# First products of small blocks in two halves of their columns, in an attention and mixture-of-experts kernel

## The chip, the core and the metric

The kernel runs on one core of a Trainium2 chip. The metric is the device time of one execution in microseconds. A core has five engines with a program each: TensorE (PE: matrix products, and PEld: loads of their weights), VectorE (DVE), ScalarE (ACT), GpSimd (POOL) and SyncE (SP, which issues most transfers). An engine runs its program in order and waits on counters (semaphores) for the others. PEldq and ACTq are the engines' sequencers.

## The reference

Two stages, in float32:

```
attn = sigmoid(q @ k.T / sqrt(64) - log(448)) @ v     # 8 x 12 heads of 448 x 64
x = attn, laid out as 3584 tokens x 768
for the tokens with x @ w_skip > 0:
    e = argmax(x @ w_gate) of 8 experts, g = its softmax weight
    x += g * (relu(x @ w1[e]) @ w2[e])                 # w1 768 x 1024, w2 1024 x 768
```

## The kernel before

After attention the tokens are sorted by expert into blocks. A loop of 14 rounds (`tc.For_i`, line 1553) takes one block a round and picks one of four arms by a word from `slots` (`choose`, 1541 to 1550):

- FULL and SPLIT take 128 rows. Each weight is held as a high and a low part, and a product is three matmuls: first product line 516, turning of h line 530, second product line 547. SPLIT belongs to the last full block of an expert and also splits the next expert's raw weights: high parts by ACT (lines 1252 and 1258), low parts by DVE.
- HALF takes up to 64 rows and FEW up to 32, at an expert's end. They use the raw float32 weights (`raw1`, `raw2`) and lay two (HALF, 64 columns each) or four (FEW, 32 each) products side by side on PE (matmuls of lines 1474 and 1416).

The order is written out by hand (`tc.manual_schedule`): each engine's program follows the text. By the start of their first product in the trace, the rounds are SPLIT 313.64, HALF 332.25, FULL 344.48, HALF 363.03, FULL 375.25, FEW 393.81, FULL 400.80, FEW 419.36, FULL 426.34, FEW 444.90, SPLIT 451.91, FEW 470.42, FULL 477.46, FEW 496.00. One HALF and one FEW follow a SPLIT, one HALF and four FEW a FULL.

A small block runs so: the first product `xf @ w1` into the bank `ph[0]`, six steps j of 128 input rows each; ACT's relu into `hs`, in column pieces (lines 1433, 1489); loads of the next w1 (`load_w1`, SP); six turns of the next block's rows `xn` on PE (`turn_x`, line 492, into `pxt`); the turns of h on PE (lines 1442, 1497) into `pht[0]` and `ph[1]`; ACT's copies of these to `ht` (lines 1444, 1503); `ready_x`, which makes the next block's `xh`, `xl` and `xf`; the second product into `py`, from `ht` and `raw2`; the weighting, the scatter of the rows, and the records of the next block. `ph[0]` and `ph[1]` are tiles of their own, `pht[0]` and `pht[1]` two banks of one tile, `pht2`. `xf` is written by ACT (`whole_x`, line 1116).

The program of PE is aligned once, ahead of the loop, by `addr_align` (line 1158), to a place in a fetch block of instructions.

Of the kernel before, what the change touches and what calls it, by code (L numbers as in the profile page):

```python
# [14 lines left out]
AF = mybir.ActivationFunctionType  # L15
# [4 lines left out]
P = 128  # L20
# [3 lines left out]
def kernel(  # L24
# [11 lines left out]
    nc = tc.nc  # L36
# [11 lines left out]
    NK1 = DM // P  # L48
    NK2 = FF // P
    H1 = FF // 2  # L50
# [6 lines left out]
    SM = 32  # L57
# [15 lines left out]
    ident = const.tile([P, P], F32, name="ident")  # L73
# [174 lines left out]
    def new_t(name):  # L248

        if ps_t is None:  # L250
            return new_s(name)[:, 0, :]
        return ps_t.tile([P, 512], F32, tag="t", name=name)
# [236 lines left out]
    def turn_x(x, h, px):  # L489
        for j in range(3):  # L490
            i = 3 * h + j
            nc.tensor.transpose(  # L492
                px[:, j * P : (j + 1) * P], x[:, i * P : (i + 1) * P], ident
            )
# [192 lines left out]
    for n, (b, hp) in enumerate(steps):  # L687
# [39 lines left out]
        for c in range(4):  # L727
            at = wk.tile([P, 2, S], F32, tag="A", name=f"at_{b}_{hp}_{c}", bufs=5)
# [83 lines left out]
    def new_ph(j):  # L812
        one = new_s(f"b{j}_ph")
        return [one[:, 0, :], ps_b.tile([P, 512], F32, tag="b", name=f"b{j}_ph1")]
# [4 lines left out]
    def turn0(h):  # L819
        pt = new_t(f"b0_pht{h}")  # L820
        for j in range(4):
            nc.tensor.transpose(
                pt[:, j * P : (j + 1) * P], hs0[h][:, j * P : (j + 1) * P], ident
            )
        split_h(h, pt, hh0, hl0)
# [28 lines left out]
    ph = new_ph(0)  # L854
# [13 lines left out]
    xf = rows_pool.tile([P, NK1, MD], F32, name="xf")  # L868
    ys = rows_pool.tile([P, DM], F32, name="ys")
    ht = rows_pool.tile([P, 4 * P], F32, name="ht")  # L870
    hs = rows_pool.tile([P, FF], F32, name="hs")
# [202 lines left out]
    ph = new_ph(1)  # L1074
# [49 lines left out]
    def ready_x():  # L1124
        for h in range(2):
            hi_x(h, pxt[h], xh)
        for h in range(2):
            whole_x(h, [slice(j, j + 1) for j in range(3)])
        for h in range(2):
            lo_x(h, pxt[h], xh, xl)  # L1130
# [24 lines left out]
    for j in range(2):  # L1155
        gemm2(j, hh0, hl0, py)
    turn0(1)
    nc.tensor.addr_align(bass.FETCH_BLOCK_INSTRUCTIONS, offset=0, max_nops=0)
    for j in range(2, NK2 - 3):
        gemm2(j, hh0, hl0, py)  # L1160
    pxt = [ps_b.tile([P, 512], F32, tag="b", name="pxt0"), new_t("pxt1")]
# [60 lines left out]
    raw1 = [[raw1g[h, i // 3][:, i % 3, :] for h in range(2)] for i in range(NK1)]  # L1222
    raw2 = [raw2g[j // 2][:, j % 2, :] for j in range(NK2)]

    ph = [new_t(f"ph{h}") for h in range(2)]
    py = new_s("py")
    pht2 = new_s("pht")
    pht = [pht2[:, h, :] for h in range(2)]

    def next_expert(word):  # L1230
        return word & (NE - 1), (word & (2 * NE)) >> (2 * NE).bit_length() - 1

    def load_w1(g, h, nx):
        return nc.sync.dma_start(
            raw1g[h, g],
            w1[ds(nx[0], 1), g * 3 * P : (g + 1) * 3 * P, h * H1 : (h + 1) * H1].rearrange(
                "o (i p) f -> p (o i) f", p=P
            ),
            cond=nx[1],
        )  # L1240
# [42 lines left out]
    def fetch():  # L1283


        pool.tensor_tensor(xn[:, 0:1], xn[:, 0:1], zf, op=ALU.add)
        pool.tensor_tensor(jk, rn[:, 0:2], rn[:, 0:2], op=ALU.add)
        pool.tensor_copy(ri, rn[:, 1:2])
        pool.tensor_tensor(rn[:, 0:1], rn[:, 0:1], zf, op=ALU.add)
        pool.tensor_tensor(rx, rix[:, 5:6], zero, op=ALU.add)  # L1290
        pool.tensor_tensor(rp[1], ri, zero, op=ALU.add)
        pool.tensor_tensor(rq, rp[1], zero, op=ALU.add)
        got = gather(xn, rp[1])

        tc.declare_no_dep(got.ins, group="put", across_iterations=True, reason="a token is in one block only")
        tc.add_to_no_dep_group("got", got.ins)
        gather_rec(rn, rx)

    def shift(eng):
        for to, src in ((riv, rix[:, 6:NS]), (rix[:, 5 : NS - 1], riv)):  # L1300
            if eng is pool:
                eng.tensor_tensor(to, src, zero.to_broadcast([P, NS - 6]), op=ALU.add)
            else:
                eng.tensor_copy(to, src)
# [39 lines left out]
    def take_rec():  # L1344

        nc.vector.tensor_copy(recs[:, 2, 0:2], rn[:, 0:2])
# [61 lines left out]
    def few(i, word):  # L1408

        nx = next_expert(word)  # L1410
        for o in range(2):
            nc.vector.tensor_copy(gate2[o * SM : (o + 1) * SM], recs[:SM, 0, 0:1])  # L1412
        take_rec()

        def quarter(dst, g, n, a, w, j, most):
            nc.tensor.matmul(  # L1416
                dst[g * SM : (g + 1) * SM, :n],
                a,
                w,
                start=(j == 0),  # L1420
                stop=(j == most - 1),
                tile_position=(0, g * SM),
            )

        Q1 = FF // 4
        for j in range(NK1):
            for g in range(4):
                s = slice((g % 2) * Q1, (g % 2 + 1) * Q1)
                quarter(ph[0], g, Q1, xf[:, j, :SM], raw1[j][g // 2][:, s], j, NK1)
        turned = (pht[0], ph[1])  # L1430
        parts = [slice(c * P, (c + 1) * P) for c in range(2)]
        for s in parts:
            nc.scalar.activation(hs[:, s], ph[0][:, s], AF.Relu)
        for h in range(2):
            for g in range(2):
                load_w1(g, h, nx)
        for h in range(2):
            turn_x(xn, h, pxt[h])
        fetch()
        ht4 = ht[:, : 8 * SM].rearrange("p (c g t) -> p c g t", c=2, g=4)  # L1440
        for s, p in zip(parts, turned):
            nc.tensor.transpose(p[:, :P], hs[:, s], ident)
        for s, p in zip(parts, turned):
            nc.scalar.activation(ht[:, s], p[:, :P], AF.Copy)
        ready_x()
        shift(dve)

        for n, j in enumerate((0, 2, 1, 3)):
            for g in range(4):
                h, o = g // 2, g % 2  # L1450
                m = j + h * (NK2 // 2)
                quarter(
                    py[:, 0, :],
                    g,
                    H2,
                    ht4[:, j % 2, 2 * h + j // 2, :],
                    raw2[m][:, o * H2 : (o + 1) * H2],
                    n,
                    NK2 // 2,
                )  # L1460
        for g in range(4):
            load_w2(g, nx)
        nc.scalar.activation(yh, py[MD:, 0, :H2], AF.Copy, scale=gate2)
        nc.vector.scalar_tensor_tensor(yt, py[:MD, 0, :H2], gate2, yh, op0=ALU.mult, op1=ALU.add)
        put(SM)
        advance()

    def half(i, word):

        nx = next_expert(word)  # L1470
        take_rec()

        def side(dst, g, n, a, w, j, most):
            nc.tensor.matmul(  # L1474
                dst[g * MD : (g + 1) * MD, :n],
                a,
                w,
                start=(j == 0),
                stop=(j == most - 1),
                tile_position=(0, g * MD),  # L1480
            )

        for j in range(NK1):
            for h in range(2):
                side(ph[0], h, H1, xf[:, j, :], raw1[j][h], j, NK1)
        turned = (pht[0], ph[1])
        parts = [slice(0, 2 * P), slice(2 * P, 4 * P)]
        for s in (slice(0, P), slice(P, 2 * P), parts[1]):
            nc.scalar.activation(hs[:, s], ph[0][:, s], AF.Relu)
        for h in range(2):  # L1490
            for g in range(2):
                load_w1(g, h, nx)
        for h in range(2):
            turn_x(xn, h, pxt[h])
        fetch()
        for c in range(4):
            nc.tensor.transpose(
                turned[c // 2][:, (c % 2) * P : (c % 2 + 1) * P],
                hs[:, c * P : (c + 1) * P],
                ident,  # L1500
            )
        for s, p in zip(parts, turned):
            nc.scalar.activation(ht[:, s], p[:, : 2 * P], AF.Copy)
        ready_x()
        shift(dve)

        ht8 = ht.rearrange("p (c h t) -> p c h t", c=4, h=2)
        for n in range(NK2):
            c, h = divmod(n, 2)
            m = h * (NK2 // 2) + c  # L1510
            for o in range(2):
                side(
                    py[:, 0, :],
                    o,
                    H2,
                    ht8[:, c, h, :],
                    raw2[m][:, o * H2 : (o + 1) * H2],
                    n,
                    NK2,
                )  # L1520
        for g in range(4):
            load_w2(g, nx)
        for o in range(2):
            s = slice(o * H2, (o + 1) * H2)
            weigh_sum(ys[:MD, s], py[o * MD : (o + 1) * MD, 0, :H2], recs[:MD, 0, 0:1])
        put(MD)
        advance()
# [56 lines left out]
```

## Time and profile before

| what | value |
|---|---|
| time, median of 3 runs | 514.08 us (513.99 to 514.44) |
| the profiled execution | 514.12 us |
| its span, mean granted clock of TensorE | 512.4 us, 0.993 |
| PE busy in the span | 499.9 us, 98% |
| ACT, DVE, POOL busy | 271.8, 294.5, 258.8 us |
| first product of a FEW (start to the first turn of xn) | 2.72 us at 419.36, 2.81 us at 470.42 |
| first product of a HALF | 5.30 us at 332.25 and at 363.03 |
| second product of a FEW, of a HALF | 2.90, 5.38 us |

A row of the timeline has the start and the length in us, the engine, the line, the operation, out<-in by the program's names (buffer numbers left out) and the shapes; in brackets stands how long the engine was idle before and what released it. A span is that of the profiled execution on the chip; the time of the run has some 1.7 us around it.

### The profile page before, as it was taken

To read this page: it belongs to the slowest core of one execution; us is meant where nothing else is said; L and a number is where in the kernel's file an instruction comes from. 1 tells how busy PE (TensorE), PEld (TensorE's weight loads), DVE (VectorE), ACT (ScalarE), POOL (GpSimd) and SP (SyncE) were. 2 spreads that over 40 slices of the span, in tenths; PEclk is the share of its full clock that TensorE was granted. 3 is DMA by queue.
4 is the path that set the end of the run, shared out by engine and by line. 5 is a ranking of instruction groups with operands and counts; after the bars stand their busy time and mean duration, and the time that the engine had idled before them with its cause. 6 is when DMAs were issued, how large, how long until landed. Compare 5 with 4: busy or idle time off the path is not lost. (4 is left out here: it accounts for less than half of the span.)

```text
span 512.4 us, 15271 instructions
## 1 busy us (share of the span) xinstructions
PE 499.9 (98%) x4982; PEld 335.9 (66%) x4983; DVE 294.5 (57%) x745; ACT 271.8 (53%) x480; POOL 258.8 (51%) x405
## 2 busy tenths in 40 slices
PE   8999999999999999999999999999999999999992
PEld 5665555555555555555557988948678787878781
DVE  5565756647868688687785842962132222249432
ACT  5776776767667677677664212933212323259322
POOL 5523455443565786657775341444223434347644
PEclk9999999999999999999999999999999999999997
DMA  7799586677698977897845035979393969697953
GB/s 231 189 235 257 144 205 158 151 172 210 168 240 235 234 198 200 214 261 193 216 99 110 2 95 166 367 226 333 90 373 119 312 246 309 253 315 254 329 214 50
DMA packets 139716, 107.27 MB, mean 209 GB/s; under 512 B 96263, under 2 KB 112265, under 8 KB 139664
## 3 DMA queue, kind: packets, MB, share of 16 engines
q1 hardware_dynamic: 133264, 97.66, 64.5%
q0 software_dynamic: 4736, 8.66, 7.0%
q8 instruction: 33, 0.54, 0.4%
q10 hardware_dynamic: 1664, 0.26, 0.3%
q14 instruction: 19, 0.16, 0.1%
HBM read 98.49 MB, written 17.60 MB: 227 GB/s over the span
## 5 line engine op out<-in xcount | busy, mean ns | idle before, releaser
L256 ACT ACTIVATE at<-s,bias 128x896 f32<-128x896 f32 (+1 forms) x191 | 170.8, 914 | 77.7 <-PE s L236 76.8
L264 PE MATMUL pa<-at,v 64*64 64x448 f32 (+1 forms) x1528 | 161.8, 490 | 0.0
L236 PE MATMUL s<-x 64*64 64x448 f32 (+1 forms) x1504 | 160.6, 494 | 0.3 <-DVE x L216 0.2
L180 POOL COPY kq<-kq 32x896 f32<-32x896 f32 (+1 forms) x96 | 88.0, 917 | 83.7 <-DMA kq<-in_q_dram 41.2
L236 PEld LDWEIGHTS s<-x 64*64 64x64 f32 x1504 | 78.0, 191 | 52.1 <-ACT at L256 20.4
L264 PEld LDWEIGHTS pa<-at,v 64*64 64x64 f32 x1528 | 61.0, 133 | 55.7 <-issue 46.9
L216 DVE STREAM_TRANSPOSE x<-kq 128x448 f32<-128x448 f32 x94 | 82.0, 946 | 4.2 <-POOL kq L180 4.2
L274 DVE TENSOR_TENSOR xt<-xt,pa 128x448 f32<-128x448 f32 x48 | 29.7, 620 | 60.8 <-ACT xt L684 59.5
L486 POOL TENSOR_TENSOR wl<-wr,wh 128x384 fp32r<-128x384 f32 (+1 forms) x28 | 31.3, 1123 | 21.1 <-DVE wh L485 18.9
L413 POOL DMA_INDIRECT lst<-rec,idx x32 | 32.5, 1016 | 13.8 <-DVE nf L923 6.0
L525 ACT ACTIVATE hs<-ph 128x512 f32<-128x512 f32 x14 | 8.4, 598 | 45.9 <-PE ph L516 38.0
L279 DVE STREAM_TRANSPOSE y<-xt 128x448 f32<-128x448 f32 x48 | 31.0, 645 | 1.7
L547 PE MATMUL py<-wh,hh 128*128 128x384 f32 x112 | 31.2, 349 | 0.0
L547 PE MATMUL py<-wl,hh 128*128 128x384 f32 x112 | 29.9, 338 | 0.0
L547 PE MATMUL py<-wh,hl 128*128 128x384 f32 x112 | 29.8, 337 | 0.0
L536 DVE TENSOR_TENSOR hl<-pht,hh 128x512 fp32r<-128x512 f32 x14 | 9.7, 690 | 33.5 <-ACT hh L535 32.2
L516 PE MATMUL ph<-wl,xh 128*128 128x512 f32 x84 | 26.6, 403 | 0.0
L684 ACT ACTIVATE xt<-pa 128x448 f32<-128x448 f32 x48 | 25.7, 536 | 1.2 <-PE pa L264 1.2
L516 PE MATMUL ph<-wh,xh 128*128 128x512 f32 x84 | 25.7, 403 | 0.0
L1349 DVE TENSOR_SCALAR ys<-py,recs 128x384 f32<-128x384 f32 (+1 forms) x18 | 10.4, 612 | 26.0 <-PE py L547 20.8
L502 DVE TENSOR_TENSOR xl<-pxt,xh 128x384 fp32r<-128x384 f32 x30 | 15.3, 552 | 16.5 <-issue 6.5
L516 PE MATMUL ph<-wh,xl 128*128 128x512 f32 x84 | 24.4, 395 | 0.0
(292 smaller groups left out, 683.5 us busy)
## 6 DMA issues: line engine op xcount, KB each, us to landing
raw<-in_moe_w_dram SPq DMA_DIRECT2D x64, 768.0 KB
v<-in_v_dram SPq DMA_DIRECT2D x47, 256.0 KB
out_dram<-y SPq DMA_DIRECT2D x192, 56.0 KB
kq<-in_k_dram SPq DMA_DIRECT2D x23, 448.0 KB
kq<-in_q_dram SPq DMA_DIRECT2D x23, 448.0 KB
wr<-in_moe_w_dram SPq DMA_DIRECT2D x12, 256.0 KB
wr<-in_moe_w_dram SPq DMA_DIRECT2D x16, 192.0 KB
lst<-fill SPq DMA_DIRECT2D x4, 464.0 KB
```

What stands on the lines that cost most here:

```text
L180: nc.gpsimd.tensor_copy(a[to, :, :, :BT], a[at, :, :, BT:])
L216: nc.vector.transpose(xs[:, n].rearrange("p (r j) -> p j r", j=NJ), t.rearrange("p (j d) -> p j d", d=D)[:, :, :BT],)
L236: nc.tensor.matmul(sc[m * D : (m + 1) * D, j, : qs.stop - qs.start], xs[r, 0, first::NR7], xs[r, 1, qs], start=True, stop=True,)
L256: nc.scalar.activation(at[:, :, :n], sc[:, :, :n], AF.Sigmoid, bias=bias, scale=SCALE)
L264: nc.tensor.matmul(pa[j * D : (j + 1) * D, r, qs], vt[r][j][:, c if r == j else (c + 1) % NV, :], at[rs, j, : qs.stop - qs.start], start=( ...
L274: nc.vector.tensor_tensor(x, x, pa[:, 1, :S], op=ALU.add)
L279: nc.vector.transpose(y, xts[b][:, hp, :])
L413: put = nc.gpsimd.indirect_dma_start(out=lst[:, :], out_offset=bass.IndirectOffsetOnAxis(ap=idx[:, c : c + 1], axis=0), in_=rec[:, c, :], ...
L486: nc.gpsimd.tensor_tensor(lo, r, hi, op=ALU.subtract)
L516: nc.tensor.matmul(ph[h], a[:, j * P : (j + 1) * P], w[j][h], start=(n == 0), stop=(n == len(t) - 1),)
L547: last = nc.tensor.matmul(py[:, o, :H2], a[h][:, js], w[j][:, o * H2 : (o + 1) * H2], start=(j == 0 and n == 0), stop=(j == NK2 - 1 and n ...
L684: nc.scalar.activation(xts[b][:, hp, :], pa[:, 0, :S], AF.Copy)
```

## The change

Three things. The program's alignment ahead of the loop goes from slot 0 to slot 172 of a block of instructions. The first product of a small block is made in two halves of its columns: all six steps j for the first half into `ph[0]`, then all six for the second into `ph[1]`, each with its relu behind it. And the first half of h is turned ahead of `turn_x`, the second half behind it, both into the two banks of `pht2`; ACT's two copies come from these.

```
-    nc.tensor.addr_align(bass.FETCH_BLOCK_INSTRUCTIONS, offset=0, max_nops=0)
+    nc.tensor.addr_align(bass.FETCH_BLOCK_INSTRUCTIONS, offset=172, max_nops=0)
...
         Q1 = FF // 4
-        for j in range(NK1):
-            for g in range(4):
-                s = slice((g % 2) * Q1, (g % 2 + 1) * Q1)
-                quarter(ph[0], g, Q1, xf[:, j, :SM], raw1[j][g // 2][:, s], j, NK1)
-        turned = (pht[0], ph[1])
+        turned = pht
         parts = [slice(c * P, (c + 1) * P) for c in range(2)]
-        for s in parts:
-            nc.scalar.activation(hs[:, s], ph[0][:, s], AF.Relu)
+        for c, s in enumerate(parts):
+            for j in range(NK1):
+                for g in range(4):
+                    at = (g % 2) * Q1 + c * P
+                    quarter(ph[c], g, P, xf[:, j, :SM], raw1[j][g // 2][:, at : at + P], j, NK1)
+            nc.scalar.activation(hs[:, s], ph[c][:, :P], AF.Relu)
+        nc.tensor.transpose(turned[0][:, :P], hs[:, parts[0]], ident)
         for h in range(2):
             for g in range(2):
                 load_w1(g, h, nx)
...
             turn_x(xn, h, pxt[h])
         fetch()
         ht4 = ht[:, : 8 * SM].rearrange("p (c g t) -> p c g t", c=2, g=4)
-        for s, p in zip(parts, turned):
-            nc.tensor.transpose(p[:, :P], hs[:, s], ident)
+        nc.tensor.transpose(turned[1][:, :P], hs[:, parts[1]], ident)
         for s, p in zip(parts, turned):
             nc.scalar.activation(ht[:, s], p[:, :P], AF.Copy)
         ready_x()
...
-        for j in range(NK1):
-            for h in range(2):
-                side(ph[0], h, H1, xf[:, j, :], raw1[j][h], j, NK1)
-        turned = (pht[0], ph[1])
+        def turn_piece(c):
+            nc.tensor.transpose(
+                turned[c // 2][:, (c % 2) * P : (c % 2 + 1) * P],
+                hs[:, c * P : (c + 1) * P],
+                ident,
+            )
+
+        turned = pht
         parts = [slice(0, 2 * P), slice(2 * P, 4 * P)]
-        for s in (slice(0, P), slice(P, 2 * P), parts[1]):
-            nc.scalar.activation(hs[:, s], ph[0][:, s], AF.Relu)
+        for s, one, pieces in zip(parts, ph, ((slice(0, P), slice(P, 2 * P)), (slice(0, 2 * P),))):
+            for j in range(NK1):
+                for h in range(2):
+                    side(one, h, 2 * P, xf[:, j, :], raw1[j][h][:, s], j, NK1)
+            for p in pieces:
+                nc.scalar.activation(hs[:, s][:, p], one[:, p], AF.Relu)
+        for c in range(2):
+            turn_piece(c)
         for h in range(2):
             for g in range(2):
                 load_w1(g, h, nx)
         for h in range(2):
             turn_x(xn, h, pxt[h])
         fetch()
-        for c in range(4):
-            nc.tensor.transpose(
-                turned[c // 2][:, (c % 2) * P : (c % 2 + 1) * P],
-                hs[:, c * P : (c + 1) * P],
-                ident,
-            )
+        for c in range(2, 4):
+            turn_piece(c)
         for s, p in zip(parts, turned):
             nc.scalar.activation(ht[:, s], p[:, : 2 * P], AF.Copy)
         ready_x()
```

Two places of the programs show what moves. A row is one instruction: its line, its operation, out<-in by the program's names with the tile's number, the size, and in brackets the counters that it waits for (`_own` are counts inside the loop, `_49` those of the rest of the program).

The first place is ACT's program in a FEW block, from the relu (line 1433) to the copies of the turned h (line 1444). Before:

```order
L1433 ACTIVATE hs<-ph_4442 128x128 [waits Activation_I-4475_own,PE_I-4475_own,Activation_49]
L1433 ACTIVATE hs<-ph_4442 128x128
L1444 REGISTER_ALU
L1444 ACTIVATE ht<-pht 128x128 [waits DVE_I-4475_own,PE_I-4475_own]
L1444 REGISTER_ALU
L1444 ACTIVATE ht<-ph_4443 128x128 [waits PE_I-4475_own]
```

With the change:

```order
L1433 ACTIVATE hs<-ph_4442 128x128 [waits Activation_I-4475_own,PE_I-4475_own,Activation_49]
L1433 REGISTER_ALU
L1433 ACTIVATE hs<-ph_4443 128x128 [waits PE_I-4475_own]
L1444 REGISTER_ALU
L1444 ACTIVATE ht<-pht 128x128 [waits DVE_I-4475_own,PE_I-4475_own]
L1444 ACTIVATE ht<-pht 128x128
```

The second relu has a wait of its own for PE now, and the second copy has none any more: one wait, at the first copy, stands for both.

The second place is PE's program in a HALF block, from the last step j of the first product (line 1474) over the turns of xn (line 492) to the first turns of h. Before (turns of h: line 1497):

```order
L1474 MATMUL ph_4442<-raw_0_1_4415,xf 64x512 [waits Activation_I-4475_own,Activation_49]
L1474 MATMUL ph_4442<-raw_1_1_4436,xf 64x512
L492 REGISTER_ALU
L492 MATMUL pxt_4368<-ident,xn 128x128 [waits DVE_I-4475_own,Pool_I-4475_own,DMASW0_I-4475_own,DMASW7_49,DVE_49]
L492 MATMUL pxt_4368<-ident,xn 128x128 x2
L492 REGISTER_ALU
L492 MATMUL pxt_4369<-ident,xn 128x128 [waits DVE_I-4475_own,DVE_49]
L492 MATMUL pxt_4369<-ident,xn 128x128 x2
L1497 REGISTER_ALU
L1497 MATMUL pht<-ident,hs 128x128 [waits Activation_I-4475_own,DVE_49]
```

With the change (turns of h: line 1484), from the last step of the first half of the columns, the second half's rows but its first two left out:

```order
L1474 MATMUL ph_4442<-raw_0_1_4415,xf 64x256 [waits Activation_I-4475_own,Activation_49]
L1474 MATMUL ph_4442<-raw_1_1_4436,xf 64x256
L1474 MATMUL ph_4443<-raw_0_0_4414,xf 64x256 [waits PE_49]
L1474 MATMUL ph_4443<-raw_1_0_4435,xf 64x256
...
L1484 MATMUL pht<-ident,hs 128x128 [waits DVE_I-4475_own,Activation_I-4475_own,DVE_49]
L1484 REGISTER_ALU
L1484 MATMUL pht<-ident,hs 128x128 [waits Activation_I-4475_own]
L492 REGISTER_ALU
L492 MATMUL pxt_4368<-ident,xn 128x128 [waits DVE_I-4475_own,DMASW0_I-4475_own,Pool_I-4475_own,DMASW7_49]
```

Each of the six steps j has its wait for ACT's count in the first half of the columns; all six stand ahead of the second half, whose steps have none. Two turns of h stand ahead of the turns of xn, two behind them.

## The prediction

> **What bounds the kernel now.** I read the page first (busy shares and the chain that ended last), then the stretches of the loop over the mixture's blocks, then the timelines of the small blocks.
>
> ```profile
> PE 499.9 (98%) x4982; PEld 335.9 (66%) x4983; DVE 294.5 (57%) x745; ACT 271.8 (53%) x480; POOL 258.8 (51%) x405
> PE 28%; issue 2%; DVE 1%; DVEq 1%; POOLq 0%; POOL 0%; ACT 0%
> 400.00:410.00 10.00, 10.00 (x55) 7.67 (x48) 2.60 (x11) 1.77 (x3) 4.26 (x8) 1.00 0.99 323
> ```
>
> PE is busy in 98% of the span, the chain that ended last lies nearly all on it where it could be followed, and in a stretch of 10 us of the loop PE works all 10.00 us at a granted clock of 1.00. No other engine is near its limit there (ACT 1.77, DVE 2.60). So a delay of PE in any block goes straight to the end, and a gain too. What matters is the order and the waits on PE in the seven small blocks. Here is a FEW block that follows a FULL one, by time (start, length, engine, line):
>
> ```profile
> 419.36 2.80 PE L1416 MATMUL ph<-raw,xf 128*32 128x256 f32 x48
> 422.08 0.88 PE L492 MATMUL pxt<-ident,xn 128*128 128x128 f32 x6
> 422.38 0.45 ACT L1433 ACTIVATE hs<-ph 128x128 f32<-128x128 f32 x2 [8.11 <-PE ph L1416]
> 422.80 0.30 PE L1442 MATMUL pht<-ident,hs 128*128 128x128 f32 x1
> 423.02 0.30 PE L1442 MATMUL ph<-ident,hs 128*128 128x128 f32 x1
> 423.14 0.28 ACT L1444 ACTIVATE ht<-pht 128x128 f32<-128x128 f32 x1 [0.31 <-PE pht L1442]
> 423.36 0.28 ACT L1444 ACTIVATE ht<-ph 128x128 f32<-128x128 f32 x1
> 423.51 2.90 PE L1416 MATMUL py<-raw,ht 128*32 128x384 f32 x32 [0.19 <-DVE gate L1412]
> ```
>
> The chain is: first product, six turns of xn (0.72 us, 0.12 each), first turn of h at 422.80, ACT's copy of it at 423.14, done at 423.42, and the second product at 423.51. The second copy ends after that start and is needed later. So the second product starts 0.71 us after the start of the first turn of h; the row's label of DVE names the semaphore nearest in time, while ACT's copy ends 0.09 before and is the operand. Between 423.02 and 423.51 PE has nothing to start: that is the gap, of which the change could take some away. There are five FEW blocks (48 matmul records of the first product in each) and two HALF blocks:
>
> ```profile
> L1416 PE MATMUL ph<-raw,xf x240: 376/379/404, 393.8 to 498.4; 128*32 128x256 f32 x120
> 363.03 5.37 PE L1474 MATMUL ph<-raw,xf 128*64 128x512 f32 x24
> 368.33 0.88 PE L492 MATMUL pxt<-ident,xn 128*128 128x128 f32 x6
> 369.04 0.38 PE L1497 MATMUL pht<-ident,hs 128*128 128x128 f32 x2
> 369.94 5.38 PE L1474 MATMUL py<-raw,ht 128*64 128x384 f32 x32
> ```
>
> **The tail of a FULL's follower.** The change takes one turn (HALF: two) ahead of the turns of xn. That helps only if ACT's first copy starts on its own turn. In the built order it does not: both turns now write the two banks of one tile, and only the first copy has a wait for PE, the second has none (the rows shown with the change). The wait is therefore for the last turn, which stands behind xn's. Before, the targets were two tiles, and each copy waited for its own. The second product's start after the change: eight turns at 0.12 put the last one's start at 422.08 + 7 x 0.12 = 422.92, where the awaited one started at 422.80 before; + 0.71 as before: 423.63, that is +0.12. In a HALF the awaited turn was the eighth (the second of the pair at 369.04) and becomes the tenth: +0.24. The ends: 0 if the early turn slips into the change from first product to turns, 0.35 if the last copy's wait also costs a sequencer's step more.
>
> **The first product in halves** does the same columns in twice the passes: 24 records in a FEW become 48 of half the length and so on. PE's time per pass of 128 columns is bounded below by half of the present one (2.72 us from 419.36 to 422.08, over 24 half passes: 0.113) and above by the 0.12 of xn's turns, which move as many columns and load four times as much weight: 24 x 0.12 = 2.88, +0.16. The first half of the passes asks for its semaphores twice as fast; the last of them stood some 1.05 after the start (row below), and the last of six steps of 0.227 is now due at 5 x 0.227 = 1.13, so it is hidden by a hair. I take +0.03 for a FEW and nothing for a HALF, whose steps are longer. The cover is PE's queue; without it a FEW would lose some 0.1 us.
>
> ```profile
> L1416 PEldq EVENT_SEMAPHORE  x6: 51/51/51, 419.5 to 420.4; - x6
> ```
>
> Sum for four FEW blocks behind a FULL: 4 x (0.12 + 0.03) = +0.6; the HALF behind a FULL: +0.24.
>
> **The two small blocks that follow a SPLIT** cost more, and it is no intended effect. Each of the six steps j of the first product waits for a count of ACT's instructions of the block before. Those counts are ACT's last six, whichever block it was. Behind a FULL these are the short copies of x into xf, done long before. Behind a SPLIT they are the last conversions of w2, and these end while the small block runs:
>
> ```profile
> 329.80 3.07 ACT L1258 ACTIVATE wh<-raw 128x768 fp32r<-128x768 f32 x4
> 334.04 1.58 ACT L1258 ACTIVATE wh<-raw 128x768 fp32r<-128x768 f32 x2 [1.18 <-issue]
> L1474 PEldq EVENT_SEMAPHORE  x6: 51/51/51, 332.2 to 335.7; - x6
> 332.25 5.37 PE L1474 MATMUL ph<-raw,xf 128*64 128x512 f32 x24
> 337.55 0.87 PE L492 MATMUL pxt<-ident,xn 128*128 128x128 f32 x6
> 338.26 0.38 PE L1497 MATMUL pht<-ident,hs 128*128 128x128 f32 x2
> 339.16 5.38 PE L1474 MATMUL py<-raw,ht 128*64 128x384 f32 x32
> ```
>
> PE's last semaphore comes at 335.7, at the end of ACT's last conversion (334.04 + 1.58 = 335.62), not some 1.05 us after the start as in the FEW above. Before, it was hidden: the steps take 5.30 / 6 = 0.88 us, so step 5 was due at 332.25 + 5 x 0.88 = 336.67. Now all six steps pass over the first columns at 0.44, and step 5 is due at 332.25 + 5 x 0.44 = 334.46, but may start at 335.7 only: PE stands for 1.24 us, with the second columns queued behind the waiting step, in order. Then 7 half steps remain, 335.7 + 7 x 0.44 = 338.79 in place of 337.55: +1.24, and with the tail +1.48. The same in the FEW behind the second SPLIT:
>
> ```profile
> 468.72 3.80 ACT L1258 ACTIVATE wh<-raw 128x768 fp32r<-128x768 f32 x5
> L1416 PEldq EVENT_SEMAPHORE  x6: 51/51/51, 470.5 to 472.6; - x6
> 470.42 2.88 PE L1416 MATMUL ph<-raw,xf 128*32 128x256 f32 x48
> 473.23 0.88 PE L492 MATMUL pxt<-ident,xn 128*128 128x128 f32 x6
> 474.63 2.90 PE L1416 MATMUL py<-raw,ht 128*32 128x384 f32 x32 [0.19 <-ACT ht L1444]
> ```
>
> ACT's five end at 472.52, the last semaphore at 472.6, and this block's first product already lost 0.09 (2.81 to the turns against 2.72). Now 7 half steps of 0.227 follow: 472.6 + 1.59 = 474.19 in place of 473.23, +0.96, with the tail +1.08. The ends: ACT's conversions do not move, as nothing ahead of them changes, so only the rest behind them is open: 0.9 to 1.5 in the HALF, 0.7 to 1.2 in the FEW.
>
> **Alignment.** The loop's code on PE starts at another slot of an instruction block. Its worth would be fetches of code that stand in the loop. The page has 33 packets of q8 over the whole span, and in the window from 330 to 505 only these two queues move anything:
>
> ```profile
> q8 instruction: 33, 0.54, 0.4%
> q1 hardware_dynamic: 16253, 38.08, 59.9%
> q0 software_dynamic: 3023, 6.35, 15.7%
> ```
>
> So no code is fetched now, and I cost it at 0. The code grows with the halves (some 140 slots by my count of the built program), and with the new offset it still spans four blocks of 256, where the old offset would need five. The cover is that all of it stays on the engine.
>
> [...]
>
> **Sum.** 0.6 + 0.24 + 1.48 + 1.08 = +3.4 us. The profiled execution took 514.12 us (span 512.4), the median is 514.08, so they are one: 514.1 + 3.4 = 517.5. By the lower ends, 0 + 0 + 0.9 + 0.7 = +1.6: 515.7; by the upper ends, 5 x (0.16 + 0.12) + 2 x 0.35 + 1.5 + 1.2 = +4.8, and a FEW's 0.1 of lost cover on top of each: 519.4.
>
> **Rivals.** What a measurement of this kernel tells from no change is about 0.2%, 1.03 us.
>
> (A) *The first copy starts on its own turn*, for then the tail gains in all seven small blocks. Relu's second part would end near 422.66 (422.38 + 0.28), the copy 0.28 and 0.09 later, the second product would start near 423.1 rather than 423.51: -0.4; at best right behind the eighth turn, 423.0: -0.5. With the two stalls as above (+1.24 + 0.96): 514.1 - 2.8 + 2.3 = 513.6, no difference; it ends below 513.1, faster, only from 0.47 us in each block on, or if the SPLIT's conversions do not bind, 511.3. For it: the gap is there in the rows. Against it: the second copy has no wait of its own, so the first one must stand for both. Chance 0.05 faster, 0.04 same.
>
> (B) *The stalls do not come*, because the count that PE waits for is reached earlier than its semaphore rows suggest (six rows, of which I place only the last). Then the tails and passes remain: 514.1 + 0.6 + 0.24 + 0.24 + 0.15 = 515.3, barely slower or the same. For it: in the kernel before, the wait is nearly free. Against it: the last semaphore stands within 0.1 us of ACT's end in both blocks, and far from it behind a FULL. Chance 0.09, of which 0.04 within 0.2%.
>
> (C) *Dearer code or passes.* The grown loop no longer stays on the engine: a fetch of about 1 us in some of 14 rounds, up to 528; or passes of 128 columns that do not halve (0.15 in place of 0.113: 5 x 24 x 0.04 = +4.5 on the forecast, 522); at worst PE spends as long on each record as now, 2.72 / 48 = 57 ns, and the five first products take twice their time, +13.6: 531. For it: the queue is asked twice as often. Against it: the turns of xn pass 128 columns in 0.12, and these are one record each, so the records' share of the time cannot be read off a FEW alone. Chance 0.06, of which 0.01 for the worst.
>
> [...]
>
> **How the numbers follow.** Forecast (tails later, two stalls): 0.76; A 0.09; B 0.09; C 0.06. Time 517.5. The forecast's own range is 515.7 to 519.4; to hold 8 in 10 it goes a little into B below: 515.5 to 519.6. Faster 0.05 (A). Same 0.09: A's 0.04, B's 0.04, 0.01 of the forecast's low end. Slower 0.86.
>
> **What would show it.** In the changed trace: the HALF near 332 shows PE standing before 335.7 with its first turn near 338.8; the FEW near 474 likewise; in FEW blocks behind a FULL the first copy to ht starts after the turn behind xn's, and the second product comes 0.1 us later than before, counted from the block's start; q8 stays at 33 or so. A first copy that starts while xn is turned makes A right and me wrong; a HALF behind the SPLIT as long as the one behind the FULL makes B right; a first product of a FEW above 3.2 us, or rows of q8 in the loop, C.

## The result, and the profile after

The changed kernel took 517.73 us (median of 4 runs, 517.40 to 517.99) against 514.22 us before on the same chip (513.99 to 514.44): a ratio of 1.0063, with a 95% interval of 1.0051 to 1.0075. That is slower by 3.5 us, close to the 517.5 that was forecast. The trace shows that two terms of that sum were wrong and made up for each other.

The page of the changed kernel is as full of PE as before, and PE's busy time has hardly grown (499.9 us in a span of 512.4 before):

```profile
span 516.3 us, 15835 instructions
PE 500.4 (97%) x5270; PEld 344.7 (67%) x5271; DVE 295.7 (57%) x745; ACT 271.7 (53%) x480; POOL 258.2 (50%) x405
```

Of the 3.9 us more of span, then, 0.5 are PE's busy time and 3.4 are time in which PE stands. The starts of the blocks in the two profiled executions (PE's timelines) say where; a block's length is the distance to the next one's start, and the last block runs to the end of the span (differences are of unrounded starts):

| block | before, us | after, us | more | forecast |
|---|---|---|---|---|
| start of the first block in the loop | 313.64 | 315.25 | +1.60 | 0 |
| HALF behind the SPLIT | 12.22 | 12.61 | +0.38 | +1.48 |
| HALF behind a FULL | 12.23 | 12.52 | +0.30 | +0.24 |
| FEW behind a FULL, three and the last | 6.99, 6.99, 7.01, 16.40 | 7.18, 7.17, 7.17, 16.38 | +0.51 | +0.60 |
| FEW behind the SPLIT | 7.04 | 8.25 | +1.21 | +1.08 |
| FULL and SPLIT, seven | 18.51 to 18.61 | 18.51 to 18.55 | -0.12 | 0 |
| sum | | | +3.88 | +3.40 |

The first line was costed at nothing. PE's timeline has a gap of 1.33 us ahead of the first product of the first block, and the rows of the branch that leads to its arm (instructions of line 1554, in the kernel before of line 1548: count, shortest/median/longest in ns, first and last start) show why. After, then before:

```profile
315.25 0.47 PE L516 MATMUL ph<-wh,xh 128*128 128x512 f32 x1 [1.33 <-issue]
L1554 PEldq COMPARE_BRANCH  x8: 73/198/2203, 312.9 to 469.9; - x8
```

```profile
L1548 PEldq COMPARE_BRANCH  x8: 73/196/255, 312.7 to 467.2; - x8
```

PE's sequencer stood 2.20 us in one branch, the first of its eight, at 312.9; the longest before took 0.26. The queue of instruction fetches, q8, shows what it stood for. Its packets have 16.4 KB each (33 with 0.54 MB on the page). While 27 of them came in the kernel before, from 12.3 to 275.9 us, PE and PEld ran 3441 and 3433 instructions, 255 a packet beside those of the sequencer itself: by this estimate one packet is one of the blocks of 256 of which the prediction speaks. In the kernel before, the last packet of q8 ahead of this branch starts at 306.1, 6.6 us before it. In the changed one it starts at 312.7, only 0.2 us before it, and takes 0.9 us; the branch ends 1.4 us behind the packet's end. In the four other runs below with a stop at the entry, the branch ends 1.40 to 1.44 us behind the end of such a packet too, however early or late that lies.

The HALF behind the SPLIT, by PE's and ACT's timelines of the changed kernel:

```profile
333.76 5.48 PE L1474 MATMUL ph<-raw,xf 128*64 128x256 f32 x48
339.17 0.44 PE L1484 MATMUL pht<-ident,hs 128*128 128x128 f32 x2
341.05 5.38 PE L1474 MATMUL py<-raw,ht 128*64 128x384 f32 x32 [0.57 <-issue]
331.32 4.53 ACT L1258 ACTIVATE wh<-raw 128x768 fp32r<-128x768 f32 x6
```

Its first product takes 5.41 us to the first turn (5.30 before): the stall that I forecast is not there. ACT's six conversions run without a break and end at 335.85, 2.09 us after the block's start, where before they waited 1.18 us for a transfer and ended 3.37 after it. The stop at the loop's entry pushed the SPLIT back by 1.6 us, SP issued the transfers as early as ever (the first of the round at 313.94, 313.84 before), and this one was done in time. The FEW behind the second SPLIT has no such help:

```profile
473.10 1.94 PE L1416 MATMUL ph<-raw,xf 128*32 128x128 f32 x40
475.34 1.74 PE L1416 MATMUL ph<-raw,xf 128*32 128x128 f32 x56 [0.31 <-ACT wh L1258]
470.65 4.54 ACT L1258 ACTIVATE wh<-raw 128x768 fp32r<-128x768 f32 x6
```

After 40 records (five of six steps over the first columns) PE waits for ACT's conversion, and the first product takes 3.91 us to the turn at 477.01. In a FEW behind a FULL the tail is as forecast (PE's and ACT's timelines):

```profile
421.68 2.90 PE L1416 MATMUL ph<-raw,xf 128*32 128x128 f32 x96
424.51 0.33 PE L1434 MATMUL pht<-ident,hs 128*128 128x128 f32 x1
425.33 0.27 PE L1442 MATMUL pht<-ident,hs 128*128 128x128 f32 x1
426.01 2.90 PE L1416 MATMUL py<-raw,ht 128*32 128x384 f32 x32 [0.41 <-ACT ht L1444]
425.64 0.45 ACT L1444 ACTIVATE ht<-pht 128x128 f32<-128x128 f32 x2 [0.60 <-DVE gate L1412]
```

The first half of h is turned at 424.51, and ACT's first copy starts only at 425.64, right behind the last turn; the second copy follows it at once (one row, two instructions). The second product starts 4.33 us after the block's start, 4.15 before. The label of the copy's row names DVE's `gate`, which had just ended; but in the FEW behind the SPLIT `gate` comes only at 479.76, and the copy there starts at 478.14, again 0.31 us after the start of the last turn. So the turn sets it.

### The profile page after: what moved, and what is told of

The parts are those of the page before. It is cut to its first block, busy times and chain, and to the rows that moved or that the text cites. A ratio compares the mean times of both kernels' runs of the same rounds, so it can differ in the third digit from the quotient of the medians.

```text
span 516.3 us, 15835 instructions
## 1 busy us (share of the span) xinstructions
PE 500.4 (97%) x5270; PEld 344.7 (67%) x5271; DVE 295.7 (57%) x745; ACT 271.7 (53%) x480; POOL 258.2 (50%) x405
## 4 chain that ended last, share of the span: by engine, by line
PE 93%; issue 2%; DVE 2%; ACT 1%; POOL 0%; POOLq 0%; DVEq 0%; ACTq 0%
PE s L236 25%; PE pa L264 24%; PE ph L516 12%; PE py L547 11%; PE py L1416 3%; PE b_py L547 2%; PE b_ph L516 2%; PE py L1474 2%; PE ph L1474 2%; PE ph L1416 2%; PE pxt L492 2%; PE pl L296 2%; PE pht L530 1%; ACT at L256 1%; PE idle L621 1%
```

## The experiments

### The alignment alone

```
     turn0(1)
-    nc.tensor.addr_align(bass.FETCH_BLOCK_INSTRUCTIONS, offset=0, max_nops=0)
+    nc.tensor.addr_align(bass.FETCH_BLOCK_INSTRUCTIONS, offset=172, max_nops=0)
```

> The kernel before with the one line of the alignment changed (slot 172 in place of 0) and nothing else. Theory A, formed after the result: the changed kernel's PE stands 1.33 us at the entry to the loop, since its second branch there took 2.20 us (0.25 before) while a block of code was fetched; the loop's head now begins just behind a block's edge, so the block with the SPLIT arm is asked for too late. Then this kernel has the same stop: time 514.2 + 1.4 = 515.6, a gap of 1.2 to 1.5 us on PE ahead of the SPLIT's first product near 315, and that branch above 2 us. Theory B: the stop belongs to the changed loop's greater code, not to the offset: no gap, 514.2 within 0.5. The one HALF behind the SPLIT and everything later keep their lengths under both.

Measured: 516.55 us (515.24 to 517.5) against 514.70 before; ratio 1.0043 (1.0026 to 1.0059). The branch and the first product of the loop in its trace:

```profile
L1548 PEldq COMPARE_BRANCH  x8: 73/194/1642, 313.1 to 468.4; - x8
314.88 0.48 PE L516 MATMUL ph<-wh,xh 128*128 128x512 f32 x1 [0.78 <-PE b_py L547]
```

The stop comes with the slot alone, in the old, shorter loop. In the profiled execution (the fastest of the four, 515.24) it is 0.78 us of PE, less than forecast, and the branch 1.64, below the 2 us expected; the median says +1.9. The packet of q8 starts 0.7 us ahead of the branch here, 0.2 in the changed kernel, so less of the fetch is left to wait for. All blocks behind it keep their lengths (HALF 12.23 each, FEW 6.99 to 7.03), and ACT's wait for its transfer in the SPLIT shrinks from 1.18 to 0.23 us, as a later SPLIT would have it. Theory A holds, with a price that is not the same in every run.

### The changed kernel with the old slot

```
-    nc.tensor.addr_align(bass.FETCH_BLOCK_INSTRUCTIONS, offset=172, max_nops=0)
+    nc.tensor.addr_align(bass.FETCH_BLOCK_INSTRUCTIONS, offset=0, max_nops=0)
```

> The changed kernel with the alignment put back to slot 0, all else as changed. By my count of the built program the SPLIT arm then starts at slot 532, in the block after the next from the loop's head, where the unchanged loop has it at 486, in the next one. Theory A (the stop at the entry is the fetch of a block that was not asked for early enough): the stop is here too, at least as long (1.3 to 2 us on PE near 314), the HALF behind the SPLIT is again hardly delayed (first product 5.3 to 5.5 us), time 517.5 to 518.3. Theory B (offset 0 keeps the entry free, as in the kernel before): no gap at the entry, ACT's conversions of w2 in the SPLIT then wait for their transfer again and the HALF's first product is 6.4 to 6.7 us long; time 517.3 to 517.8. The two differ in the trace more than in the time. Any fetch of code after 340 would show a loop over five blocks that does not stay on the engine; I expect none.

Measured: 523.14 us (522.82 to 524.94), far above both expectations; ratio to before 1.0163 (1.0146 to 1.0180). Branches, the two gaps on PE, the stretches around the first, with the granted clock (third number from the right), and fetches of code after 330:

```profile
L1554 PEldq COMPARE_BRANCH  x8: 73/202/3967, 312.9 to 476.9; - x8
316.42 0.76 PE L516 MATMUL ph<-wh,xh 128*128 128x512 f32 x1 [2.44 <-issue]
339.15 6.19 PE L1474 MATMUL ph<-raw,xf 128*64 128x256 f32 x39 [2.80 <-ACT wh L1258]
316.40:319.50 3.10, 3.08 (x8) 2.47 (x9) 0.00 (x0) 0.00 (x0) 0.09 (x1) 0.51 1.00 339
319.50:322.00 2.50, 2.50 (x12) 2.05 (x11) 0.00 (x0) 0.00 (x0) 0.00 (x0) 1.00 1.02 387
q8 instruction: 1, 0.02, 0.0%
```

The first branch stands for 3.33 us (the row of the window around it has one branch of 3327 ns) and leaves PE idle for 2.44 us; then the branch out of that SPLIT stands 3.97 us and leaves it idle for 2.80, which the row puts down to ACT although ACT's last conversion (six in a row from 333.85 for 4.54 us) had ended at 338.39, 0.76 before. Behind each of the two gaps TensorE ran at half the clock for some 3 us (0.51 in the row above; 0.50 in the stretch from 341 to 343). That was in neither theory, and the HALF's first product, 7.11 us at that clock, decides between them no more. The packet of q8 that the first branch waits for starts 0.7 us after the branch has begun, where in the other stops it starts 0.2 to 0.7 us ahead. So for the grown loop the new slot is the better of the two, by some 5 us, and for the old loop the old one, by 1.9: an alignment has no worth of its own apart from the code behind it. That the block of code in which the first arm stands decides it fits my count of the built programs, but only three slots were measured. One fetch only lies after 330, so this loop, which by that count spans five blocks, stays on the engine too once it has run: q8 has no packet from 336 to 510.

### The changed kernel with the entry free

```
-    nc.tensor.addr_align(bass.FETCH_BLOCK_INSTRUCTIONS, offset=172, max_nops=0)
+    nc.tensor.addr_align(bass.FETCH_BLOCK_INSTRUCTIONS, offset=205, max_nops=0)
```

> The changed kernel with the alignment at slot 205: the edge of a block then lies some 42 slots ahead of the loop's head, about as the code before it takes several us, and the SPLIT arm starts in the next block. Theory A: no stop at the entry (under 0.2 us), the SPLIT starts near 313.7. My prediction's own step for the HALF behind it then comes back: ACT's last two conversions of w2 wait for their transfer up to about 334, as in the kernel before, and the HALF's first product takes 6.4 to 6.7 us in place of 5.41. The 1.4 us saved at the entry are given back there: 517.3 to 517.9, no difference to the changed kernel (517.73). Rival: the two terms are independent, the HALF stays at 5.4 and the time falls by the whole stop, to 516.3.

Measured: 517.19 us (516.46 to 518.70); ratio to before 1.0044 (1.0028 to 1.0061). Branch, ACT's last conversions and the HALF behind the SPLIT:

```profile
L1554 PEldq COMPARE_BRANCH  x8: 73/192/242, 313.7 to 470.5; - x8
334.87 1.58 ACT L1258 ACTIVATE wh<-raw 128x768 fp32r<-128x768 f32 x2 [1.19 <-issue]
333.06 1.95 PE L1474 MATMUL ph<-raw,xf 128*64 128x256 f32 x16
335.86 3.98 PE L1474 MATMUL ph<-raw,xf 128*64 128x256 f32 x32 [0.85 <-ACT wh L1258]
339.76 0.44 PE L1484 MATMUL pht<-ident,hs 128*128 128x128 f32 x2
```

No branch above 0.25 us, no gap at the entry. ACT waits 1.19 us for its transfer again, PE stops after four steps (16 records) for ACT's conversion, and the first product takes 6.70 us: +1.29 over the changed kernel. From the first product in the loop to the end of the span it is 202.30 us here and 201.04 in the changed kernel: 1.26 more, where the missing stop saves 1.33. The stop and this stall stand in for each other. The rival, that the HALF stays at 5.4, falls by the trace; the times alone (516.46 to 518.70, and a ratio whose interval reaches down to 1.0028) would not tell it from the theory.

### The one tile alone

```
-        turned = (pht[0], ph[1])
+        turned = pht
```

(both arms of the kernel before, nothing else)

> The kernel before with one edit in each small arm: the turned h goes into the two banks of the one tile in place of one bank of it and another tile; first product whole and turns behind the turns of xn as before. Theory (one tile, one wait): the first copy waits for the last turn. In a FEW the last turn starts 0.22 us after the first (423.02 against 422.80), in a HALF the awaited one is the fourth in place of the second, some 0.38 later: 5 x 0.22 + 2 x 0.38 = +1.9, 516.1. Rival (the copies go on starting by their own turns, and the tail of the changed kernel has another cause): 514.2 within 0.4.

Measured: 515.90 us (515.49 to 516.29, 10 runs); ratio 1.0022 (1.0012 to 1.0032). A FEW in it:

```profile
424.38 0.49 PE L1442 MATMUL pht<-ident,hs 128*128 128x128 f32 x2
424.90 0.45 ACT L1444 ACTIVATE ht<-pht 128x128 f32<-128x128 f32 x2 [0.51 <-PE pht L1442]
425.28 2.90 PE L1416 MATMUL py<-raw,ht 128*32 128x384 f32 x32 [0.41 <-DVE recs L1346]
```

The first copy starts 0.52 us after the first turn (0.34 before), behind the second one, and the two copies run as one. FEW blocks grow by 0.12 to 0.19 (0.22 expected: the second turn now follows the first without a break), HALF blocks by 0.40 each (0.38 expected). That is +1.5 in all from the loop's first product on; the times give +1.2. The rival falls: the shared tile has a price of its own.

### The turns in two tiles again

```
-        turned = pht
+        turned = (pht[0], ph[0])
```

(both arms of the changed kernel)

> The changed kernel (slot 172) with one edit in each small arm: the second half of h is turned into the bank ph[0] (free since the first relu) in place of the other bank of the one tile; order and halves as changed. In the program the first copy then waits for its own turn only. Theory: in a FEW the second product starts about 1.0 us after the end of the first product in place of 1.51 (it was 1.43 before the change), since relu's second part ends at +0.6, the first copy 0.28 later; in a HALF 1.2 to 1.3 in place of 1.88 (before: 1.61). Sum 5 x -0.5 + 2 x -0.6 = -3.7: 514.0, the entry's 1.3 us and the FEW's stall behind the SPLIT left in. Rival (the tail is set by the sequencer or by ACT's order, not by the shared tile): tails within 0.1 of the changed kernel's, 517.3 or more.

Measured: 515.50 us (514.21 to 516.28, 10 runs); ratio to before 1.0014 (1.0004 to 1.0024). A FEW behind a FULL, and ACT ahead of the FEW behind the SPLIT:

```profile
421.99 0.33 PE L1434 MATMUL pht<-ident,hs 128*128 128x128 f32 x1
422.43 0.27 ACT L1444 ACTIVATE ht<-pht 128x128 f32<-128x128 f32 x1
422.81 0.27 PE L1442 MATMUL ph<-ident,hs 128*128 128x128 f32 x1
423.01 2.46 PE L1416 MATMUL py<-raw,ht 128*32 128x384 f32 x28
470.51 1.58 ACT L1258 ACTIVATE wh<-raw 128x768 fp32r<-128x768 f32 x2 [0.46 <-SPq L1554]
```

The first copy now starts at 422.43, ahead of the last turn, and the second product follows the turns at once: 1.02 us after the first product's end (1.51 in the changed kernel), 1.24 in a HALF (1.88). FEW blocks behind a FULL take 6.51 to 6.57 us (7.17), HALF blocks 11.88 and 11.94 (12.52 and 12.61). From the loop's first product to the end of the span it is 197.77 us in place of 201.04, -3.27 of the expected -3.7. The rest is in one block: blocks that come earlier, as it seems, leave the second SPLIT less time; its last conversions wait 0.46 us, and the FEW behind it has a first product of 4.51 us (3.91) and no gain in all. The time shows only -2.2: in these ten runs 1.7 to 3.25 us of it lie outside the span, where the changed kernel has 1.7 to 1.8; why is open.

### The steps in another order

```
-        for c, s in enumerate(parts):
-            for j in range(NK1):
+        for c, js in ((0, range(4)), (1, range(4)), (0, range(4, NK1)), (1, range(4, NK1))):
+            for j in js:
...
-            nc.scalar.activation(hs[:, s], ph[c][:, :P], AF.Relu)
+            if js[0]:
+                nc.scalar.activation(hs[:, parts[c]], ph[c][:, :P], AF.Relu)
```

(FEW; the same in HALF; slot 205)

> The changed kernel at slot 205 (no stop at the entry) with the steps of the first product in another order: 0 to 3 of the first columns, 0 to 3 of the second, then 4 and 5 of the first, 4 and 5 of the second; one tile for the turns as changed. Theory (steps 4 and 5 wait for ACT's last two conversions of w2 in the SPLIT): they are now due at 8 and 9 half steps in place of 4 and 5, near where the kernel before had them, and the stall goes: first product of the HALF behind the SPLIT 5.3 to 5.5 us (6.70 at slot 205 before this edit), of the FEW behind the SPLIT 2.9 to 3.1 (3.91). Time 517.2 - 1.3 - 0.95 = 515.0. Rival (the stall is the transfer of the weights or the halves' own pace): both first products stay as long, 517.2.

Measured: 517.64 us (516.80 to 517.75); ratio to before 1.0057 (1.0043 to 1.0072). The HALF behind the SPLIT, and ACT and PE in a FEW behind a FULL:

```profile
331.99 5.40 PE L1475 MATMUL ph<-raw,xf 128*64 128x256 f32 x48
337.32 0.44 PE L1485 MATMUL pht<-ident,hs 128*128 128x128 f32 x2
333.86 1.58 ACT L1258 ACTIVATE wh<-raw 128x768 fp32r<-128x768 f32 x2 [1.26 <-issue]
422.79 0.67 ACT L1434 ACTIVATE hs<-ph 128x128 f32<-128x128 f32 x2 [7.69 <-PE ph L1416]
423.16 0.30 PE L1435 MATMUL pht<-ident,hs 128*128 128x128 f32 x1 [0.16 <-issue]
```

As to its cause the theory holds: with ACT's conversions as late as ever (1.26 us of waiting), the HALF's first product takes 5.33 us in place of 6.70, and the FEW's behind the SPLIT 3.25 in place of 3.91. Little of it is left in the whole: in every FEW relu of the first columns now ends late, the early turn waits for it ahead of xn's turns, and the block takes 7.52 us in place of 7.17 or so. My 515.0 had left that out. From the loop's first product to the end of the span it is 201.71 us, 0.6 less than at slot 205 before this edit; the times (517.64 against 517.19, with intervals that overlap) do not show a gain.

### All of it

```
-        turned = pht
+        turned = (pht[0], ph[0])
...
-        for h in range(2):
-            turn_x(xn, h, pxt[h])
+        turn_x(xn, 0, pxt[0])
+        nc.tensor.transpose(turned[0][:, :P], hs[:, parts[0]], ident)
+        turn_x(xn, 1, pxt[1])
```

(the order of steps of the last experiment in both arms; the early turn of a FEW amid xn's; slot 205, and 172 in the run after)

> Both of these edits together at slot 205, and in a FEW the first half's turn in the middle of xn's turns (its relu ends later now). Theory: the entry free, no stall behind a SPLIT, second products 1.0 (FEW) and 1.2 us (HALF) after the first, against 1.43 and 1.61 in the kernel before: 5 x -0.4 + 2 x -0.4 + 0.1 for each first product = -2.1 to -2.8. Time about 2.4 below the kernel before of the same chip, faster by 0.4 to 0.55%. Rival: the relu of the first columns, which now ends only 0.13 us after the first product of a FEW, holds PE up again and half of it is lost: -1.2.

Measured: 513.30 us (512.05 to 513.57, 6 runs) against 514.56 before; ratio 0.9966 (0.9954 to 0.9979). Faster than both kernels, by half of what I expected against the one before. The number is the rival's, but in the rows its mechanism is not: the turn of the first half follows the turns of xn, and PE has no idle time ahead of it. A FEW behind a FULL:

```profile
421.65 0.27 PE L1439 MATMUL pht<-ident,hs 128*128 128x128 f32 x1
421.96 0.28 ACT L1445 ACTIVATE ht<-pht 128x128 f32<-128x128 f32 x1 [0.17 <-PE pht L1439]
422.08 0.27 PE L1443 MATMUL ph<-ident,hs 128*128 128x128 f32 x1
422.33 2.90 PE L1416 MATMUL py<-raw,ht 128*32 128x384 f32 x32
```

HALF blocks take 11.89 and 11.88 us (12.22 before the change), FEW blocks behind a FULL 6.67 to 7.00 (6.99). The FEW behind the SPLIT gains nothing (7.08 against 7.04), and PE loses time in two places later (0.3 us ahead of the second SPLIT, 0.35 in the FULL at 476.30). Their cause is open.

> The kernel with all of these edits, at the change's own slot 172. Theory: only the stop at the loop's entry comes back, 1.3 to 1.4 us of PE ahead of the SPLIT near 315, and as no small block waits for ACT any more, nothing of it is given back later: 1.3 to 1.5 above the kernel with slot 205. Rival (the alignment's price is hidden by what follows): within 0.4 of it.

Measured: 514.45 us (513.95 to 514.64, 11 runs); ratio to before 0.9995 (0.9986 to 1.0004). The entry in its trace:

```profile
315.03 0.48 PE L516 MATMUL ph<-wh,xh 128*128 128x512 f32 x1 [1.06 <-issue]
L1558 PEldq COMPARE_BRANCH  x8: 73/202/1862, 313.0 to 466.9; - x8
```

PE stands 1.06 us at the entry and the branch 1.86. By the medians that is +1.15 over slot 205, a little under the expected 1.3, so the stop would cost its whole length. The two profiled executions do not bear that out: their spans are 511.6 and 512.0 us, only 0.4 apart (the first is the slowest of its six runs), as the two losses of slot 205, ahead of the second SPLIT and in the FULL at 476.30, are not there: those blocks take 6.71 and 18.55 us. How much of the stop comes back here is not settled.

## Why the prediction was right, and where it was not

- **PE bounds, every wait of it goes to the end**: right. PE's busy time grew by 0.5 us, the span by 3.9.
- **The tail: one tile, one wait**: right in its cause. The one tile alone, and its removal, move the copy as the order of the waits says. +0.15 a FEW with the passes and +0.24 a HALF were forecast; the blocks grew by 0.16 to 0.19 and 0.30. In a FEW the two parts were not split rightly: from the first turn to the second product it is 0.08 more (0.12 forecast), and the passes put on 0.10 (0.03 forecast).
- **Passes of half the columns take half the time**: nearly. In a FEW 96 records to the first turn take 2.83 us, where 48 took 2.73 (the prediction's "24 records" there are 48); the worst case of rival C, records that do not shrink, is out.
- **The stall of the FEW behind the SPLIT**: right, +1.21 for +1.08, at the upper end of its 0.7 to 1.2.
- **The stall of the HALF behind the SPLIT, +1.24**: not there. The step that failed is the sentence "ACT's conversions do not move, as nothing ahead of them changes". The alignment does change something ahead: the SPLIT starts 1.6 us later, its weights' transfer does not, and ACT's wait for it is gone. With the entry free the first product takes 6.70 us in place of 5.30, +1.40 where +1.24 was costed.
- **Alignment at 0**: wrong, +1.2 to 1.9 (the medians of slot 172 against 205 and against 0; 1.33 us of PE in the profiled execution; only 0.4 between the spans of the last pair). I had looked for fetches from 330 on, and there are none in either kernel; the price lies at the entry, in the loop's first round, where the branch to the first arm took 2.20 us in place of 0.26 and ended 1.4 us behind a packet of q8. The cover was named as "all of it stays on the engine", which holds only from the second visit on.
- **The sum** came out at 517.5 by luck: +1.60 at the entry that was costed at nothing, and 1.10 of the +1.48 in the HALF that did not come. The one error fed the other: where the stop is missing, the stall takes its place.
- **Rival B** (the stalls do not come) would be right by the sign that I gave it, a HALF behind the SPLIT as long as the one behind the FULL: 12.61 against 12.52. Its reason is not what happened: the FEW behind the SPLIT stalls, and so does the HALF as soon as the entry is free. The sign could not tell the two apart.
- **Rival A** (the copy starts on its own turn) was out for this change, and right about the price: with two tiles the second product of a FEW comes 0.41 us sooner after the first than in the kernel before.

## What to carry to other kernels

Moving work ahead of a wait helps only if the wait is for that work: look at the tile, since two results in one tile can have one wait, for the later one (here 0.12 to 0.19 us in a FEW, 0.40 in a HALF). A product made in two halves of its columns needs its last input after half the time (with the entry free, the first product of the HALF behind the SPLIT went from 5.30 to 6.70 us): list what each step waits for in every order of blocks that occurs, not in the common one. An offset of code in a loop with arms can have a price of its own, here paid at the first branches of the loop (2.20 us in place of 0.26 in the changed kernel), and has to be measured anew when an arm grows. And a sum that comes out is no proof of its terms: check each one in the trace.

## What the runs showed of the hardware that was not expected

PE's branch at the loop's entry took 1.64, 1.86, 1.87, 2.20 and 3.33 us in the runs with a stop, and 0.24 to 0.26 in the others; the branch out of the first SPLIT took 3.97 once, 0.19 to 0.31 otherwise. The length goes with when the packet of q8 starts: 0.73 us ahead of the branch where it took 1.64, 0.47 to 0.48 ahead at 1.86 and 1.87, 0.17 ahead at 2.20, 0.73 behind its start at 3.33. A loop over four or five blocks (by my count of the built programs) then ran its remaining rounds with no fetch at all: q8 has no packet from 330 to 508 in the changed kernel, and none from 336 to 510 with slot 0. TensorE's granted clock fell to 0.51 for some 3 us after a stop of 2.44 us of PE; behind the stop of 1.33 us of the changed kernel it stayed at 1.00 (stretch from 315 to 318):

```profile
315.00:318.00 3.00, 2.75 (x12) 2.28 (x13) 0.09 (x1) 0.00 (x0) 1.04 (x1) 1.00 0.78 262
```

With 96 records in place of 48, of half the columns each, the first product of a FEW took 2.83 us in place of 2.73: 29 ns a record in place of 57.
